# A state-space layer and two feed-forward layers: y of one pair of chunks joined with the next pair's C·B and states, 25 weight shifts on ScalarE, and a new order

## The chip, the cores and the metric

The kernel runs on one core of one Trainium2 chip. The metric is device microseconds of one execution, without a profile, as the median of repeated runs. A second source is one profiled execution, whose hardware trace gives all the rows shown here.

## What is computed

Four sequences of 768 tokens go through a chunked state-space layer (8 heads of 32, state size 16), and its output of 3072 tokens x 256 goes through two feed-forward layers. The first is `elu(x @ w_in) @ w_out` with 2048 inner columns. The second has 1024 inner columns: `(x @ w1) * (x @ w2)`, then `@ w3 @ w_out`. The part that matters here, cut from the reference:

```python
L = exp(cum[..., :, None] - cum[..., None, :]) * causal
M = einsum('bhin,bhjn->bhij', C, B) * L
y = einsum('bhij,bhjd->bhid', M, x)
y += einsum('bhin,bhnd->bhid', C, state) * exp(cum)[..., None]
state = decay_full * state + sum_j(B x decay_from_j)
```

The weights of the feed-forward layers come as 64-bit floats.

## The kernel before

**Chunks and pairs.** The tokens are worked through in 24 chunks of 128 rows, two halves of 64 in each. Four chunks make one tile of 512 tokens. The chunks go in pairs. For each pair but the first two there are two phases of small f32 products on TensorE. `unit_u` (L658) makes C·B of both chunks (`cb_products`, L511, matmuls on L521) and the new parts of the states (`u_products`, L548, L556). `unit_y` (L670) calls `y_products` (L582): M times x (L590, the inner part), then C times state (L598, the state part). The array is divided for them: 32x64 cells for C·B, 64x32 for u and the inner part, 32x32 for the state part. The first four chunks have their own `first_cb`, `first_u` and `first_y`.

**What follows a phase.** After C·B, VectorE multiplies by the decay (`decayed`, L528) and makes the states (`states`, L565). After y, ScalarE (first two tiles) or VectorE copies the result as a rounded high part xTh (`made_x`, L685), and VectorE takes the low part xTl (`take_lo`, L162). Every large product is three matmuls (`mm3`, L382 to L384), low times high, high times low, high times high.

**Rooms in PSUM.** `banks` (L171) gives double banks out of three. A `unit_u` takes two rooms, a `unit_y` two others, and each unit of `x @ w_in` (`unit_a`, L706) one. A room comes free when its last reader is done. The stage of the second layer's `x @ w1` and `x @ w2`, made as sums of products of blocks (`by_product`, L852), has six single banks of its own; there VectorE multiplies two results (`gate_1`, L902, into room_l) and frees a bank for the next product.

**Weights.** A `Piece` (L192) loads 512 KB as pairs of 32-bit words, and makes an f32 of each pair. `shifted` (L209) takes the low word down by 29 bits on VectorE (L210), `scaled` (L213) works on the high word on ScalarE (L214), `joined` (L222) puts them together on VectorE (L224), `his` and `los` make the high and low parts (L236 on ScalarE, L162). There are 44 pieces. The sixteen of w_in and w_out come first, in an order written into `PIECES` (L55), through eight rooms that they take in turn. DMAs of all loads are issued on SP's queue, in program order.

**The order.** `ORDER` (L37) is a string of 1670 letters, written by hand or by a search. Each letter runs the next waiting step of one kind (L1040), and `in_order` (L646) keeps what it issues in that order on every engine. So the order of letters is the order of each engine's queue. The letter v is `half_a` (L701): the first 256 of 512 columns of a unit of `x @ w_in`, kept in `early_h` so that `unit_a` makes the rest alone. The test there is `early = t == 0 and n < len(early_h)`.

Of the kernel before, what the change touches and what calls it, by code (L numbers as in the profile page):

```python
# [37 lines left out]
094AAlU7AlC5Al5UCJCD566l8jCNk5K8JkHND6IjDQjND6KkHNkKQzzYNYzIvzjYNYjkaKjk!HaKXjkxIkNjKarkKMjsHMxKbIrNKxsXrLaHkBjLN8j8vsxX  # L38
BHKuWkPIrbDHMKjkIMKbWINsRXaWHLCNjLBbxCDrCttBjNsCakhVkiyxIrKbXkzsWzMHYYuhKNIaHiXIDbxDNrttjsyVaKzXzkHYYhNVaIxijMrkKbMsHxPL
raINhLjsaxijNhRbxXrLCCiaMSBSBrsBCbshxirLahKBiaxksHrIkbjsxCNKrKuHksbhItDVahtDjijykxirbMKHsMzbzhYPiNYuhKbXHtDtDjkyLaBzIzYY  # L40
INiaxKrXLHbHIsxNkhIRa1jBrMiaCxNCsrKwXxshkNribfsjCXjKHuFhMIatjDHNLIakxCDSiSr1bKxtLNrwsjskykfHFKhIaMzzHKjINibBkMBxYKYbhNri
PsuhbXjDtiXwtkDLykfhFRaHXHIziBNbxIYjLrwzBsNYKukHMfIbjFDMKtHNaDILXCkwxBLCNhtrKajsfjKhiaxiHrkIbFKHxINsrbhskyhSwPjzzYYMKiaH
XSIijMfBakxCFNHCrIaXxsrRwxsrsbfjKkFLahBiuLxbrtBDCHDItbshiKyhHbzXIzYi1CuhYMaDDXttwixMrLBafNLsbBxCFrCkNjsyhazijYkbKxzKr3Y%
&su&h=bitbhtD&D=y=S&Saz=YNziaxYrsaNh3xibxkrrbsshiahjijKbxkK%&ra&s^=hb=&ix&=ar=Nsax1rh3aNxirksb3jxKs@jakK%&=a@#&h3rib&s@&
=x=b=h#Nri^ahs^xia@N#rk#jxsbrKsaSkjSKh%b@i&=xb^h&@=#ahi&ribx#s3r1xsb&=h3^@iar=hbix/srsbh/i|ch_bmi/|#b_/G|e]_gncS[Em({|G}
)]_e>gn<c[*Em(.{G})],<e.>En,g.{*c[,(m)S}*g.1>e.,*G[<3nc,.d*](,mE.}G.{d.,<e],)ng>E,.c{[*dm,(G*.}d.<e]*,d$.d,$),ng>.d+*.(,
[dc,$E}.d@{em,<@d#nG#d*3]g@+)[#^(>E}*c@{e.<dn^dm+d@#G.,)]#*g$>E@(.#^[c{3.d}*m),.e.,G<ng>](,@^E[}c,dm,e.#g.,Gd,*]d{E+n*).
<d.{d[*,(>d)+*c}d+m<e.,2gn>3G[+(]c.}dm,E.3,d.,G.,d,*g{e<dn*)+.(]+2*d.}E.>[d{.c,<2em,).Gn*>g],d.,d.,c[E,md,*({G}*.d<]).e*
>$d,.g*n,c[d.+($,2dm,E.}G.,d]{e$,<)@+gn#d[*(>@E}.*c{e<dn#d.,^)m+d@.g#^@G>.d,@*d+@d#](^.,E[c{*dm}).#G<.>e@#dng]#c[,Em,({G
}g],).,e,*En>d[d+*.d{c<*dm,).+(.*G>.g}.d],<[e+En+2c.,dm{(d}d,G,e]<)$,g.+*dn>2[d,c*.+(.d}*.d,2mE,G*.e{d,n<).,d.>g](,[c,E}  # L50
m*d{e*dnG.)],(.>*d$}E.<g.,d.{[c,<$d+me$,2).g,d+[d>nG.d.d.+c],(mE}d,e{G,nd+]),g<(>.d$[d.Ed{}),<d>,d..,d,dd+++++
# [44 lines left out]
def kernel(  # L96
# [485 lines left out]
    def y_products(*chunks):  # L582
        for k, both in chunks:
            c = ck[k]
            for g in range(2):
                for s in range(SUB):
                    rows = slice(R * s, R * s + R)
                    for q in range(4):
                        h = 2 * q + g
                        T.matmul(both[32 * q:32 * q + 32, s, g], c["x"][rows, D * h:D * h + D], c["L"][rows, h],  # L590
                                 start=g == 0, stop=(k, s) not in state, skip_group_check=True)
        for g in range(2):
            for s in range(SUB):
                for k, both in chunks:
                    for q in range(4) if (k, s) in state else ():
                        at = turned(k, q)
                        rows = slice(32 * at, 32 * at + 32)
                        T.matmul(both[32 * q:32 * q + 32, s, g], state[k, s][rows, D * g:D * g + D], ck[k]["cd"][rows, s, g],  # L598
                                 start=False, stop=True, skip_group_check=True)
# [43 lines left out]

    ends = {}
# [68 lines left out]
    def elu(t, n, h):  # L713
# [9 lines left out]
        if not plain:  # L723
# [4 lines left out]
            yield "i"  # L728
            take_lo(V, lo, e, hi)
# [379 lines left out]
```

## Time and profile before

| | us |
|---|---|
| Median of three runs (526.65 to 526.8) | 526.7 |
| The profiled execution | 524.71 |
| Its span, first to last instruction | 523.0 |
| TensorE (PE) busy | 508.8 |
| VectorE (DVE) busy | 428.8 |
| ScalarE (ACT) busy | 323.6 |
| GpSimd (POOL) busy | 204.4 |

A span is the time from the first to the last instruction of the core. Busy is the union of an engine's instructions, and matmuls overlap, so the starts of matmuls say more of TensorE's pace than their lengths. A wait is put down to the instruction that ended it.

### The profile page before, as it was taken

Reading aid. Unit: us, or ns where it says so; the run is one execution under the profiler, and the core shown is the slowest. Engines: PE = TensorE matmul, PEld = TensorE weight load, DVE = VectorE, ACT = ScalarE, POOL = GpSimd, SP = SyncE. Lnnn points to the kernel's source line nnn. Section 1 sums busy time; section 2 is a strip of 40 time slices with the busy share of each in tenths; the row PEclk is TensorE's granted clock in tenths of the full one; section 3 lists DMA queues with packets and bytes.
Section 4 is the critical chain, followed back from the end, with each engine's and each line's share of the span. In section 5 each row is a group of like instructions: output and inputs, shape, how many; then the busy total and the mean of one; then the engine's idle time right before and its main releaser. Section 6 shows DMA issues by size and latency. Waiting matters only on the chain.

```text
span 523.0 us, 10654 instructions
## 1 busy us (share of the span) xinstructions
PE 508.8 (97%) x4330; PEld 411.2 (79%) x4330; DVE 428.8 (82%) x589; ACT 323.6 (62%) x482; POOL 204.4 (39%) x184
## 2 busy tenths in 40 slices
PE   5799999999999999999999999999989999999996
PEld 3675788778888888878788888888777888888885
DVE  6888989879897996867766797869999989988845
ACT  2585587655754385535476787747766577765650
POOL 3223004205430544122203333967477465755401
PEclk9999999999999999999999999999999999999999
DMA  8993473147555635053202321001000110001002
GB/s 297 348 277 132 134 207 126 41 143 235 170 158 150 222 108 174 1 160 104 69 35 77 106 80 47 35 0 61 0 22 21 61 41 20 1 20 41 21 1 80
DMA packets 28177, 52.66 MB, mean 101 GB/s; under 512 B 2304, under 2 KB 10880, under 8 KB 28128
## 3 DMA queue, kind: packets, MB, share of 16 engines
q1 hardware_dynamic: 27984, 51.85, 30.4%
q8 instruction: 34, 0.56, 0.4%
q14 instruction: 15, 0.12, 0.1%
q10 hardware_dynamic: 144, 0.13, 0.1%
HBM read 45.58 MB, written 6.39 MB: 99 GB/s over the span
## 4 chain that ended last, share of the span: by engine, by line
PE 91%; DVE 6%; issue 1%; DMA 0%; ACT 0%; DVEq 0%
PE acc L382 9%; PE acc L384 9%; PE h L382 9%; PE acc L383 9%; PE h L383 9%; PE h L384 9%; PE p L382 4%; PE p L384 3%; PE p L383 3%; PE acc L745 3%; PE p_d L382 2%; PE p_d L384 2%; PE p_d L383 2%; PE p_E L382 2%; PE p_E L383 2%; PE p_E L384 2%
## 5 line engine op out<-in xcount | busy, mean ns | idle before, releaser
L715 ACT ACTIVATE e<-h 128x1024 f32<-128x1024 f32 x48 | 49.2, 1025 | 58.0 <-PE h L384 55.5
L382 PE MATMUL h<-xTh,w_in 128*128 128x512 f32 (+1 forms) x200 | 80.0, 400 | 0.8 <-ACT xTh L685 0.8
L383 PE MATMUL h<-xTl,w_in 128*128 128x512 f32 (+1 forms) x200 | 77.7, 389 | 0.0
L384 PE MATMUL h<-xTh,w_in 128*128 128x512 f32 (+1 forms) x200 | 77.5, 388 | 0.0
L162 DVE TENSOR_TENSOR g<-e,g 128x1024 fp32r<-128x1024 f32 x44 | 60.1, 1370 | 15.5 <-ACT g L727 15.4
L382 PE MATMUL acc<-g,w_out 128*128 128x512 f32 x176 | 69.6, 396 | 0.0
L722 DVE SCALAR_TENSOR_TENSOR e<-e,h 128x1024 f32<-128x1024 f32 x44 | 53.3, 1214 | 19.7 <-ACT e L717 19.6
L384 PE MATMUL acc<-g,w_out 128*128 128x512 f32 x176 | 68.6, 390 | 0.0
L383 PE MATMUL acc<-g,w_out 128*128 128x512 f32 x176 | 68.5, 389 | 0.0
L727 ACT CAST g<-e 128x1024 fp32r<-128x1024 f32 x44 | 46.2, 1049 | 30.0 <-PE acc L384 26.5
L717 ACT ACTIVATE e<-e 128x1024 f32<-128x1024 f32 x48 | 50.7, 1059 | 0.8
L382 PEld LDWEIGHTS h<-xTh,w_in 128*128 128x128 f32 x200 | 38.6, 193 | 9.4 <-issue 1.8
L383 PEld LDWEIGHTS h<-xTl,w_in 128*128 128x128 f32 x200 | 38.5, 193 | 7.8 <-issue 0.7
L384 PEld LDWEIGHTS h<-xTh,w_in 128*128 128x128 f32 x200 | 38.6, 193 | 7.6
L162 POOL TENSOR_TENSOR w<-raw_wc,w 128x512 fp32r<-128x512 f32 x16 | 23.9, 1502 | 51.5 <-ACT w L236 48.6
L536 POOL TENSOR_TENSOR xbc<-xbc,pr 128x256 f32<-128x256 f32 (+1 forms) x24 | 22.9, 965 | 50.9 <-DMA L<-a_cut 30.7
L382 PEld LDWEIGHTS acc<-g,w_out 128*128 128x128 f32 x176 | 33.0, 188 | 7.4
L384 PEld LDWEIGHTS acc<-g,w_out 128*128 128x128 f32 x176 | 33.0, 188 | 7.0
L383 PEld LDWEIGHTS acc<-g,w_out 128*128 128x128 f32 x176 | 33.1, 188 | 6.6
L504 POOL TENSOR_TENSOR xbc<-xbc,L 128x128 f32<-128x128 f32 x24 | 15.1, 634 | 58.1 <-DVE L L498 37.7
L899 POOL TENSOR_TENSOR room_l<-room_l,room_o 128x512 f32<-128x512 f32 x12 | 19.8, 1647 | 32.8 <-DVE room_o L896 19.1
L498 DVE TENSOR_TENSOR_SCAN L<-L,eye 128x512 f32<-128x512 f32 x20 | 27.3, 1368 | 2.0 <-DMA L<-a_cut 2.0
(427 smaller groups left out, 1278.2 us busy)
## 6 DMA issues: line engine op xcount, KB each, us to landing
xbc<-in_xc SPq DMA_DIRECT2D x24, 512.0 KB, 6.3
raw_wc<-in_w3t SPq DMA_DIRECT2D x16, 512.0 KB, 4.3
L<-a_cut SPq DMA_DIRECT2D x40, 128.0 KB, 4.8
raw_wi<-in_w_in SPq DMA_DIRECT2D x8, 512.0 KB, 8.6
raw_wo<-in_w_out SPq DMA_DIRECT2D x8, 512.0 KB, 6.4
x_dram<-x SPq DMA_DIRECT2D x6, 512.0 KB, 4.9
room_s<-x_dram SPq DMA_DIRECT2D x12, 256.0 KB, 4.3
out_t<-out SPq DMA_DIRECT2D x11, 256.0 KB, 2.0
```

The costliest lines, as they stand in the source:

```text
L162: eng.tensor_tensor(out=lo, in0=raw, in1=hi.bitcast(F32), op=ALU.subtract)
L382: T.matmul(out, wlo, xhi, start=first, stop=False, **kw)
L383: T.matmul(out, whi, xlo, start=False, stop=False, **kw)
L384: T.matmul(out, whi, xhi, start=False, stop=last, **kw)
L498: V.tensor_tensor_scan(out=flat, data0=wide, data1=eye.rearrange("p h s -> p (h s)"), initial=0.0, op0=ALU.mult, op1=ALU.add)
L536: G.tensor_tensor(out=c["cd"][:, n:], in0=c["cd"][:, n:], in1=c["pr"].rearrange("p s (o i) -> p s o i", o=1)[:, n:].to_broadcast([P, SUB - ...
L715: A.activation(e, h, AF.Exp)
L717: A.activation(e, e, AF.Relu, scale=-1.0, bias=1.0)
L722: V.scalar_tensor_tensor(out=gt[t, n] if plain else e, in0=e, scalar=-1.0, in1=h, op0=ALU.mult, op1=ALU.max)
L727: A.copy(hi, e)
L745: T.matmul(acc, word_of(n)[:, j, es], g[:, j], start=m == 0, stop=False)
L899: GATE[m % 2].tensor_tensor(out=s["two"], in0=s["two"], in1=s["u2"], op=ALU.mult)
```

## The change

The y of a pair now takes the whole room that the next pair's C·B and states would have had, and where `JOINED` has a 1 (six of ten pairs of chunks), `unit_u` writes into that same room, and the new `ORDER` has it follow `unit_y` at once. `y_products` makes the state part first, chunk by chunk, and the inner part after it. `unit_u` makes u first and C·B after it. 25 of 44 pieces have their low word shifted by ScalarE. The pieces of w_in and w_out come in another order, and the string `ORDER` is new (the same letters, the same number of each). `POOL_LO` is all zeros and `SCALAR_Z` keeps the old value, so these two change nothing.

```diff
+JOINED = "0100111101"
+SCALAR_Z = 2
+SCALAR_LOW = "11101000001101011001111011011010111100101010"
-PIECES = [(("w_in", "w_out")[k == "o"], "iioiooiiiiooiooo"[:n].count(k)) for n, k in enumerate("iioiooiiiiooiooo")] + [("wo2", m) for m in range(4)] + [("w3", m) for m in range(16)] + [
+PIECES = [(("w_in", "w_out")[k == "o"], "iiioioioiooioioo"[:n].count(k)) for n, k in enumerate("iiioioioiooioioo")] + [("wo2", m) for m in range(4)] + [("w3", m) for m in range(16)] + [
...
         def shifted(self):
-            V.tensor_scalar(self.low, self.low, 29, None, op0=ALU.logical_shift_right)
+            if self.scalar_low:
+                A.activation(self.low, self.low, AF.Copy, scale=15 / 16 * 2.0 ** -29 * (1 - 2.0 ** -8))
+            else:
+                V.tensor_scalar(self.low, self.low, 29, None, op0=ALU.logical_shift_right)
             self.one_of_two()
...
     def y_products(*chunks):
         for k, both in chunks:
+            for g in range(2):
+                for s in range(SUB):
+                    for q in range(4) if (k, s) in state else ():
+                        at = turned(k, q)
+                        rows = slice(32 * at, 32 * at + 32)
+                        T.matmul(both[32 * q:32 * q + 32, s, g], state[k, s][rows, D * g:D * g + D], ck[k]["cd"][rows, s, g],
+                                 start=g == 0, stop=False, skip_group_check=True)
+        for k, both in chunks:
             c = ck[k]
             for g in range(2):
                 for s in range(SUB):
...
-        for g in range(2):
-            for s in range(SUB):
-                for k, both in chunks:
-                    for q in range(4) if (k, s) in state else ():
...
     def unit_u(k):
...
-        rooms = {j: parts_of(banks(f"s{j}")) for j in two}
-        cb_products(*((j, rooms[j][0]) for j in two))
+        rooms = {j: parts_of(joined[j] if JOINED[(k - CPT) // 2] == "1" else banks(f"s{j}")) for j in two}
         for j in two:
             u_products(j, rooms[j][1])
+        cb_products(*((j, rooms[j][0]) for j in two))
...
     def unit_y(k):
-        two = [(j, by_head(banks(f"y{j}")[:, :, :2 * R])) for j in (k, k + 1)]
+        joined.update({j + 2: banks(f"y{j}") for j in (k, k + 1)})
+        two = [(j, parts_of(joined[j + 2])[2]) for j in (k, k + 1)]
...
-094AAlU7AlC5Al5UCJCD566l8jCNk5K8JkHND6IjDQjND6KkHNkKQzzYNYzIvzjYNYjkaKjk!HaKXjkxIkNjKarkKMjsHMxKbIrNKxsXrLaHkBjLN8j8vsxX
+094AAlA75AlUl5UCJCl566kD5jN8DJjCDQ686KNk8jDCkK!NHkKjIHKNQzzYHYNIzvzYkYNjIajkKvMxKkjakPHKrIaNkxsMrLbjMsxjKNrLajXkHsMKjbIH
```

Three places of the order show what the prediction speaks of. The first is on TensorE, the y of chunks 10 and 11 in the kernel before (y10 and y11 are rooms, st states, L the decays):

```order
L590 MATMUL y10_1434<-L10_988,xbc10_940 32x64 x16
L590 MATMUL y11_1435<-L11_1079,xbc11_1059 32x64 x16
L598 MATMUL y10_1434<-xbc10_940,st6_850 32x64 x4
L598 MATMUL y11_1435<-xbc11_1059,st7_853 32x64 x4
L598 MATMUL y10_1434<-xbc10_940,st10_1424 32x64 x4
L598 MATMUL y11_1435<-xbc11_1059,st11_1428 32x64 x4
L598 MATMUL y10_1434<-xbc10_940,st6_850 32x64 x4
L598 MATMUL y11_1435<-xbc11_1059,st7_853 32x64 x4
L598 MATMUL y10_1434<-xbc10_940,st10_1424 32x64 x4
L598 MATMUL y11_1435<-xbc11_1059,st11_1428 32x64 x4
```

The same y with the change, and what stands right behind it:

```order
L597 MATMUL y10_1440<-xbc10_1014,st6_799 32x64 x4
L597 MATMUL y10_1440<-xbc10_1014,st10_1408 32x64 x4
L597 MATMUL y10_1440<-xbc10_1014,st6_799 32x64 x4
L597 MATMUL y10_1440<-xbc10_1014,st10_1408 32x64 x4
L597 MATMUL y11_1441<-xbc11_1033,st7_828 32x64 x4
L597 MATMUL y11_1441<-xbc11_1033,st11_1415 32x64 x4
L597 MATMUL y11_1441<-xbc11_1033,st7_828 32x64 x4
L597 MATMUL y11_1441<-xbc11_1033,st11_1415 32x64 x4
L606 MATMUL y10_1440<-L10_1007,xbc10_1014 32x64 x16
L606 MATMUL y11_1441<-L11_1054,xbc11_1033 32x64 x16
L564 MATMUL y10_1440<-xbc12_1268 32x64 x8
L564 MATMUL y11_1441<-xbc13_1313 32x64 x8
```

The state part now stands ahead of the inner part, and all of chunk 10 ahead of all of chunk 11, where the two took turns by four. The u and C·B of chunks 12 and 13 follow at once, into the rooms y10 and y11; before, some hundred rows lay between.

The second is on TensorE after the unit of `x @ w_in` number 3 of the first tile, before the change (w_in1 is the weight piece of unit 1):

```order
L382 MATMUL h0_3_490<-xTh0_364,w_in3_81 128x512
L383 MATMUL h0_3_490<-xTl0_365,w_in3_81 128x512
L384 MATMUL h0_3_490<-xTh0_364,w_in3_81 128x512
L382 MATMUL h0_1_517<-xTh0_364,w_in1_79 128x256
L383 MATMUL h0_1_517<-xTl0_365,w_in1_79 128x256
L384 MATMUL h0_1_517<-xTh0_364,w_in1_79 128x256
L382 MATMUL h0_1_517<-xTh0_364,w_in1_79 128x256
L383 MATMUL h0_1_517<-xTl0_365,w_in1_79 128x256
```

And with the change, after unit 0 of the first tile:

```order
L390 MATMUL h0_0_381<-xTh0_370,w_in0_78 128x256
L391 MATMUL h0_0_381<-xTl0_371,w_in0_78 128x256
L392 MATMUL h0_0_381<-xTh0_370,w_in0_78 128x256
L390 MATMUL h0_1_417<-xTh0_370,w_in1_79 128x256
L391 MATMUL h0_1_417<-xTl0_371,w_in1_79 128x256
L392 MATMUL h0_1_417<-xTh0_370,w_in1_79 128x256
L390 MATMUL h0_1_417<-xTh0_370,w_in1_79 128x256
L391 MATMUL h0_1_417<-xTl0_371,w_in1_79 128x256
```

Twelve matmuls of 256 columns for unit 1, which stood behind unit 3, are now the first half of unit 1; the second half follows them, also as twelve of 256 columns, and the twelve of 512 columns are gone. Before, unit 1 had been made whole, its early half came later, and no instruction read it.

The third is on ScalarE's queue at the start, before the change, from the copies of the first states (st0) to the last part of x of the first pair:

```order
L572 COPY st0_209<-f2_138 128x128
L572 COPY st1_211<-f2_138 128x128
L214 ACTIVATE raw_wi0_121<-raw_wi0_121 128x512
L236 CAST w_in0_78<-raw_wi0_121 128x512
L572 COPY st2_248<-acc_f_96 128x128
L214 ACTIVATE raw_wi1_123<-raw_wi1_123 128x512
L214 ACTIVATE raw_wo0_125<-raw_wo0_125 128x512
L572 COPY st3_305<-acc_f_96 128x128
L236 CAST w_in1_79<-raw_wi1_123 128x512
L685 CAST xTh0_364<-f2_138 128x2x2x64
L685 CAST xTh0_364<-acc_f_96 128x2x2x64
```

And with the change, from behind the copies of st0 and st1:

```order
L216 ACTIVATE raw_wi0_121<-raw_wi0_121 128x512
L222 ACTIVATE raw_wi0_121<-raw_wi0_121 128x512
L222 ACTIVATE raw_wi1_123<-raw_wi1_123 128x512
L580 COPY st2_289<-acc_f_96 128x128
L580 COPY st3_294<-acc_f_96 128x128
L216 ACTIVATE raw_wi1_123<-raw_wi1_123 128x512
L222 ACTIVATE raw_wi2_125<-raw_wi2_125 128x512
L216 ACTIVATE raw_wi2_125<-raw_wi2_125 128x512
L244 CAST w_in0_78<-raw_wi0_121 128x512
L222 ACTIVATE raw_wo0_216<-raw_wo0_216 128x512
L244 CAST w_in1_79<-raw_wi1_123 128x512
L695 CAST xTh0_370<-f2_138 128x2x2x64
```

Three shifts (L216) stand there that were VectorE's, and the scaling of w_in2 comes ahead of the first copies of x, as that of w_out0 already did. The last row is the first of the same two copies of x; the second follows it.

## Rows read from the trace of the kernel before

**Rows 1.** The page: busy time, share and instructions of each engine

```profile
PE 508.8 (97%) x4330; PEld 411.2 (79%) x4330; DVE 428.8 (82%) x589; ACT 323.6 (62%) x482; POOL 204.4 (39%) x184
```

**Rows 2.** Waits of PE over the run: total us, times, longest us

```profile
PE f L487 <- ACT a_hl L426: 4.4, 1, 4.4
...
PE p L382 <- DVE room_l L902: 1.8, 2, 1.4
```

**Rows 3.** Windows of 20 us: length, PE, PEld, DVE, ACT, POOL busy, clock, DMA

```profile
20.00:40.00 20.00, 19.29 (x141) 15.47 (x144) 16.73 (x27) 15.88 (x25) 3.38 (x6) 1.00 0.94 288
...
360.00:380.00 20.00, 19.55 (x85) 15.42 (x84) 19.97 (x25) 14.24 (x27) 10.54 (x7) 1.00 0.04 12
380.00:400.00 20.00, 18.61 (x81) 14.72 (x80) 19.37 (x23) 13.07 (x25) 14.22 (x10) 1.00 0.09 28
```

**Rows 4.** PE timeline, first big products: start, length, instruction

```profile
20.71 0.55 PE L382 MATMUL h<-xTh,w_in 128*128 128x256 f32 x1 [0.83 <-ACT xTh L685]
...
25.36 0.33 PE L384 MATMUL h<-xTh,w_in 128*128 128x256 f32 x1
...
25.88 0.40 PE L382 MATMUL h<-xTh,w_in 128*128 128x512 f32 x1
...
37.53 0.28 PE L382 MATMUL h<-xTh,w_in 128*128 128x256 f32 x1
...
39.05 0.80 PE L521 MATMUL s<-xbc 32*64 32x128 f32 x32
```

**Rows 5.** PE timeline, a C·B and u phase, then a y phase

```profile
60.38 0.39 PE L384 MATMUL acc<-g,w_out 128*128 128x512 f32 x1
60.70 0.69 PE L521 MATMUL s<-xbc 32*64 32x128 f32 x32
61.32 0.45 PE L556 MATMUL s<-xbc 64*32 64x64 f32 x32
61.70 0.50 PE L382 MATMUL h<-xTh,w_in 128*128 128x512 f32 x1
62.04 0.40 PE L383 MATMUL h<-xTl,w_in 128*128 128x512 f32 x1
62.27 0.40 PE L384 MATMUL h<-xTh,w_in 128*128 128x512 f32 x1
...
67.39 0.86 PE L590 MATMUL y<-L,xbc 64*32 64x64 f32 x64
68.18 0.85 PE L598 MATMUL y<-xbc,st 32*32 32x64 f32 x64
68.96 0.50 PE L382 MATMUL h<-xTh,w_in 128*128 128x512 f32 x1
```

**Rows 6.** PE timeline near the start, and line 598: durations min/median/max

```profile
19.20 0.33 PE L598 MATMUL f<-xbc,st 32*32 32x64 f32 x4
19.23 0.33 PE L598 MATMUL acc_f<-xbc,st 32*32 32x64 f32 x4
19.31 0.33 PE L598 MATMUL f<-xbc,st 32*32 32x64 f32 x4
...
L598 PE MATMUL y<-xbc,st x640: 211/214/239, 56.9 to 257.9; 32*32 32x64 f32 x160
```

**Rows 7.** ScalarE timeline at the start

```profile
12.13 0.43 ACT L572 COPY st<-f 128x128 f32<-128x128 f32 x2 [7.81 <-PE f L556]
...
15.44 0.71 ACT L214 ACTIVATE raw_wi<-raw_wi 128x512 f32<-128x512 f32 x1
16.01 0.70 ACT L214 ACTIVATE raw_wo<-raw_wo 128x512 f32<-128x512 f32 x1
...
20.19 0.38 ACT L685 CAST xTh<-acc_f 128x256 fp32r<-128x256 f32 x1
```

**Rows 8.** Tile raw_wi: durations min/median/max of its two first operations

```profile
L214 ACT ACTIVATE raw_wi<-raw_wi x8: 657/679/709, 12.5 to 43.7; 128x512 f32<-128x512 f32 x8
L210 DVE TENSOR_SCALAR raw_wi<-raw_wi x8: 404/421/612, 13.3 to 53.4; 128x512 uint32<-128x512 uint32 x8
```

More of the change, by code (lines that the diff above doesn't have):

```diff
@@ L42 @@
[L42 to L51, printed above, removed]
+094AAlA75AlUl5UCJCl566kD5jN8DJjCDQ686KNk8jDCkK!NHkKjIHKNQzzYHYNIzvzYkYNjIajkKvMxKkjakPHKrIaNkxsMrLbjMsxjKNrLajXkHsMKjbIH
@@ new lines @@
+KNkBIxLXraLkNKjsaxXKHRrXbxIHCNsrCWIBW8sujCWNaDBhtBDCtkyKkjixuMKbztHNkrIDHXYjIbzthMskYjXaDhKiPLyxNLrBbzsBzHYYjNuIiaMRXbxV
+DrXtWsakMhDtNhKaVjixrVaiHxIsNbxkLrrsBaChsCSiSyjKxVbPrzzHKMYIHsbhXkLNaihBIjYMiCbxXLrBNCsuhLbiRbhkikkaKtHDjItjbDxBKNrKyHK1
+HsIuXzkIYazHDNjItYDaxMthkjNwixKrMrsbXfKHshINajikHFLIaxKNrLwxsjkNrKbkHshIHajINhKBSiCwkSCfjCFiNafxFKHrIbHsBxCyIhkurMbjsMzY
+XDatDNkiwLxhtKbNzHYriIPfajFBXjKhLNkbsiBRyhxuzCrKbjskzaiDYtbxKYrDhaHijItsbxNrhsMwki1bXHHIhXIfajFKSNCSiCaxMrkNaxKsrhwxiLbH
+sBrLfbhFBsIHjikyIhKCuPzYwDMtzYMibfHDXjtkFyKHazMLXYBRbxMrLCXaIzYsBILahxirwxsrhbsNfFiuhaDjNiD1btxkKtjkrasKax%&&hbrBi&=xbs=
@@ new lines @@
+h=Lra&S=sNaxiSrXahsxNirbBksCjCxykCjKrKuhs%bDzDaihYzt3bxYt&r=yi3&&shb&==iah=zNYibxzYajNrks3bxKrkh3sajhKi%&ax=&@irb^#&xs3r
+b1==&h=sNa@SiS1#bx^rN^@sahhika#xi^jjKa@kxK#%rb@sr&s&ah=xirb#@@#&s3b&h==x=ia3^h#ribx/srsbh/i|ch_bmi/|_b/G|e]_gnc[Em({|G})
+]_e>En<g.{*cS,([m)}.G><Se,]1g.d*n,E3[({*.c})m,*e.>G.,gnd.,[c<](,*mE}.G{g.,<)],eE>n*d{.c[,*(.d}.dm,*e.<gn,).,G$>d$](*+.d}
+[d,E$c.{d@,<dm,@)@G#*e>]3#E.*d.,nd+g*{c[d,.^d.+)m#(^@>d.}g@,c@[e#mG<d#*]gn#E[^(3.{G})],<e@>d$,3cn#Em,(.G{d}]),.e*,dn>g*(
++[d<.*c.+Em}d.{*g,e<G,n)]+d.^>(2.E+[c.}d,md.,G{g,e,)n,*d]<d>E*.+c.{2d[*,dm).+(*.>d.2}g.,3<d[+e,dnG2,c],(m,E.}*g{e,d*.d<.
+),$*dn>d[,$G*.d+](,.E}@c{$em,<.G#.)n,d]>d@,d.#g*@+c[(,m^d}g#*E@+G.{e]^#dnE@*(.{).<d^@}[d>.)<#.cem>*@g,nc[#G,d]#(.,dmE}g,
@@ L197, in __init__ @@
             self.lo, self.word, self.parts, self.half = G, None, None, 0
+            self.scalar_low = False
         def load(self):
@@ L590, in y_products @@
                         T.matmul(both[32 * q:32 * q + 32, s, g], c["x"][rows, D * h:D * h + D], c["L"][rows, h],
-                                 start=g == 0, stop=(k, s) not in state, skip_group_check=True)
-        for g in range(2):
-            for s in range(SUB):
-                for k, both in chunks:
-                    for q in range(4) if (k, s) in state else ():
[L596 to L599, printed above, removed]
+                                 start=g == 0 and (k, s) not in state, stop=True, skip_group_check=True)
     def x_room(k):
@@ L642, in first_y @@
             later("X", at_load, CPT + k)
+    joined = {}
     ends = {}
@@ L670, in unit_y @@
     def unit_y(k):
-        two = [(j, by_head(banks(f"y{j}")[:, :, :2 * R])) for j in (k, k + 1)]
+        joined.update({j + 2: banks(f"y{j}") for j in (k, k + 1)})
+        two = [(j, parts_of(joined[j + 2])[2]) for j in (k, k + 1)]
         y_products(*two)
         for j, both in two:
-            later("z", made_x, j, both, A if j < 2 * CPT else V)
+            later("z", made_x, j, both, A if j < SCALAR_Z * CPT else V)
         if k % CPT == 0 and k // CPT + 1 < NTILE:
@@ L727, in elu @@
             A.copy(hi, e)
-            yield "i"
-            take_lo(V, lo, e, hi)
+            pool = POOL_LO[t * NA + n] == "1"
+            yield "T" if pool else "i"
+            take_lo(G if pool else V, lo, e, hi)
     def split_word(n):
@@ L1010 @@
         p.lo = V if 0 < n < VECTOR_LO else G
+        p.scalar_low = SCALAR_LOW[n] == "1"
     for k in range(CPT):
```

6 lines of the change are left out of this document (3 added, 3 removed).

## The prediction

> **What bounds the kernel now.** The page's busy times come first: TensorE is busy 508.8 of 523.0 us, and no other engine over 82% [rows 1]. Then TensorE's waits: the longest are 4.4 us before its first matmul and 1.8 us, in two pieces, for VectorE's L902 [rows 2]. Those two lie between 360 and 400 us, where TensorE is busy 19.55 and 18.61 of 20 us, so that 1.84 us are lost, with VectorE busy 19.97 and 19.37 [rows 3]. The reader is to see that TensorE sets the time almost everywhere: what counts is how much it has to do, how well matmuls follow each other, and when the first large product can start. Lengths hide the second of these, since matmuls overlap, so the timeline is read by starts. Large ones of 512 columns start 0.23 us apart (62.04 to 62.27) [rows 5]. At the start, those of 256 columns take (25.36 - 20.71) / 21 = 0.22 us each, then (25.88 - 25.36) / 4 = 0.13, so TensorE goes at half its pace until 25.4 us, that is at 1.2 GHz and then at 2.4, though the granted clock reads 1.00 in that window [rows 3, 4].
>
> All sums are made against the profiled execution, 524.71 us. The three runs have a median of 526.7, 2.0 us more; I carry the same difference over to them.
>
> **Part 1: the early half of unit 1.** Between 37.53 and 39.05 stand twelve matmuls of 256 columns whose result no one reads [rows 4]. Less the entry into the next phase (0.09, Part 2) they cost 1.52 - 0.09 = 1.43 us. With the change they are used. The price is that unit 1 is now 24 of 256 columns in place of 12 of 512: 24 x 0.12 - 12 x 0.23 = 0.1 us. Sum **-1.3 us**. TensorE has no wait in that stretch that could take it back, other than what Part 4 counts.
>
> **Part 2: six joins.** A phase of small products costs something to enter and to leave. From the last large matmul to the first of C·B are 0.32 us in place of 0.23 (60.38 to 60.70): 0.09. The first large one after a phase takes 0.34 until the next one starts (61.70 to 62.04), 0.11 too much [rows 5]. And before it the array runs empty: the last matmul of L598 starts about 68.18 + 0.85 - 0.21 = 68.82, with 0.21 as the length of one [rows 6], and the next large one at 68.96, 0.14 later, where small ones start 0.02 apart or closer (64 in 0.64 us) [rows 5]. A join saves one exit and one entry, 0.09 + 0.11 + 0.12 = 0.32. From the inner part to u the cells keep their 64x32 shape, so no new gap arises there. Six joins: **-1.9 us**. Below: -1.2, if only the two neighbours of large matmuls are saved; above: -2.0. That u now goes ahead of C·B changes which shape comes last, not how many changes there are; I put nothing, within 0.1 us of each of ten phases either way, since both orders have one entry, one change and one exit.
>
> **Part 3: the state part, one chunk at a time.** This speaks against the change. Near the start, four matmuls of the first chunk (f) start at 19.20, four of the second (acc_f) at 19.23, and the next four of the first at 19.31 [rows 6]. So a cell of the array takes a new pass of 64 columns only 0.11 us after the one before, at half pace, thus 0.055 at full; and the second chunk, whose four cells are others, fits into the same time. A chunk's state part has 16 instructions on four cells, two records each (64 records for two chunks) [rows 5]: eight passes per cell, the last starting 7 x 0.055 = 0.39 after the first, 0.41 with the four side by side. Two chunks by turns needed 0.64 us from first to last start (68.18 to 68.82). One after the other they need 2 x 0.41 = 0.83, if matmuls keep their order. That is 0.19 for each of ten phases: **+1.9 us**. Below 0, if the second chunk overtakes; above +2.4, if each chunk keeps the whole 0.44 of its eight passes. I take the rows' own pace.
>
> Matmuls that keep their order are what the Trainium skill states (TensorE: Matmul & The Clock Gate, Part 3, The mechanism: strict first in, first out in start and end). TensorEngine Tiling (Array Packing), Key Properties, says that different tiles load weights and multiply in parallel; by that alone this term would be 0 and the time 522.0. No row here has a long run on one chunk's four cells, so the trace doesn't decide between them.
>
> **Part 4: the start.** The first large product waits for ScalarE's copy of x, which ends at 20.19 + 0.38 = 20.57 and lets it start at 20.71 [rows 4, 7]. ScalarE's queue up to there is now longer, but it is held up less: it had waited again and again for VectorE, which made shift, joining and scans by turns. From 12.13, where the copies of the first states start, the new queue has the two copies (0.33), nine instructions on pieces (six are shifts and scalings of w_in0 to w_in2, one scales w_out0, two are roundings), two more state copies (0.33), and the two copies of x (0.65). At 0.57 from start to start (15.44 to 16.01) [rows 7] that is 12.13 + 0.33 + 9 x 0.57 + 0.33 + 0.65 = 18.57, 2.0 us sooner. A shift on ScalarE is priced like the scaling of the same size, 0.68 us, since no row shows it [rows 8]. y must be there by then: all C·B stands ahead now, and VectorE makes its four scans and the four decays with one joining between them, so that y of the first pair is due before 17 us. Against it: the copies of states 2 and 3 wait on TensorE with the shift of w_in1 queued behind, and GpSimd makes the last of its products for C ahead of the low part of w_in0. I take **-1.5 us**, between 0 and -2.0. The half pace should last as long as before, and moves along.
>
> **Part 5: what I put at nothing.** The 25 shifts take 25 x 0.42 = 10.5 us off VectorE and put 25 x 0.68 = 17 us on ScalarE [rows 8]. Neither is waited for between 21 and 360 us by more than the 0.83 us at its start [rows 4], and ScalarE has 4.1 us idle even in the full window from 20 to 40 [rows 3]; GpSimd's subtractions for the weights follow ScalarE as before. If that cover were gone, a late rounding would cost about one instruction, 0.66, at the unit that needs it. On SP's queue w_in2 and w_in3 go ahead of w_out pieces, which helps the start; the rows of decays and the next chunks' loads come later, but their first use, the phase of chunks 4 and 5, moves back behind two more units of `x @ w_in`. The joined rooms wait for VectorE's C·B work in place of a fresh pair; see the last rival. In the stage from 360 us the order is new and VectorE as full: I leave its 1.84 us, between 0 and twice that and more.
>
> **Sum.** -1.3 - 1.9 + 1.9 - 1.5 = -2.8: 521.9 for the profiled execution, **523.9** for the median.
>
> **The rivals.**
> A: the second chunk overtakes in the state part. Then Part 3 is 0 and the time 526.7 - 4.7 = 522.0. For it: cells that start 0.03 us apart do work at once [rows 6]. Against it: the matmuls seen there already stood in that order.
> B: the product stage loses more. From 360 to 400 us VectorE has 0.66 of 40 us to spare [rows 3], and its instructions there take 0.7 us or more, so each that is placed one too early before L902 is a wait of that size. With four such, 2.8 us, the gain is gone: 526.7, within 0.2%, about what a measurement can tell from no change.
> C: joined rooms, on the slow side. Of three rooms a joined phase holds two until VectorE has made the low parts, the decays and the states of both chunks, some 3.5 to 4 us by its eight to ten instructions of 0.3 to 0.7. Cover is the rest of the phase, 1.0 us (60.70 to 61.70) [rows 5], and one unit in the third room, 12 x 0.23 = 2.7. The sum is even, so it decides whether one longer VectorE instruction of a unit stands ahead: then TensorE waits about 1 us. For it: six joins in a stretch where VectorE is 80% busy. Against it: after four of the joins a unit on the accumulators stands first, which needs no room. At all six, 6 x 0.9 = 5.4: 526.7 - 2.8 + 5.4 = 529.3.
>
> **How the numbers follow.** The forecast has 0.42, with a range of its own from 522.8 to 525.4; A has 0.25, B 0.18, C 0.15. The forecast and A are faster by over 0.2% (1.05 us, so below 525.65): 0.67. B is the same, 0.18; C slower, 0.15. The range reaches from 521.0 (A with the full gain at the start and half the waits of the product stage gone) to 527.2, which leaves out most of C.
>
> **What would show it.** Right: the first product of `x @ w_in` starts near 19.2 us; no twelve lone matmuls after unit 3; from y to u no large gap, and 14 phases in place of 20; L597's 64 records take about 0.83 us from first to last start in place of 0.64; a shift on ScalarE takes 0.6 to 0.7 us; TensorE waits for L913 (the old L902) about 2 us. Wrong: L597 still in 0.64 (then A); waits of `x @ w_in` for VectorE's L536 or L573 behind joined phases (C); waits from 340 us on above 4 us (B); a first product that starts at 20.7 or later.

## The result and the profile after

Against the kernel before on the same chip the changed kernel took 534.13 us in the median of five runs (531.18 to 534.55), the kernel before 526.65: a ratio of 1.0141, with a 95% interval from 1.012 to 1.0163. It is 7.5 us slower. The forecast was 523.9, with a range up to 527.2. The profiled execution took 531.18 us, its span is 529.5.

The page of the changed kernel: busy times, and the DMA queue that, as worked out below, carries TensorE's instructions. A queue's row has packets, MB and share.

```profile
PE 508.9 (96%) x4330; PEld 412.5 (78%) x4330; DVE 411.7 (78%) x564; ACT 336.1 (63%) x507; POOL 200.8 (38%) x184
...
q8 instruction: 34, 0.56, 0.5%
```

VectorE has lost 17 us and ScalarE gained 13 [rows 1 for before]. The shifts make the 13 and 10 of the 17: in the last experiment, which puts all of them back on VectorE, ScalarE has 12.7 less and VectorE 10.0 more than with them on ScalarE (323.3 and 423.6 against 336.0 and 413.6). TensorE has the same busy time in a span that is 6.5 us longer. So it waits, and the waits of PE say where (us in total, times, longest):

```profile
PE y L529 <- issue: 3.9, 3, 1.4
PE acc_f L606 <- issue: 2.2, 1, 2.2
PE y L564 <- issue: 1.8, 1, 1.8
PE acc_f L597 <- POOL xbc L544: 1.0, 1, 1.0
...
PE p L390 <- DVE room_l L904: 0.5, 1, 0.5
```

The wait of the product stage, which [rows 2] had at 1.8, is down to 0.5. New are waits inside joined phases (L529, L564: lines of C·B and u that write into y) and at the start (L606), and their releaser is "issue": the engine waited for nothing that the profile shows. Two joined phases on PE's timeline, the one near 56 us without such a wait and the one near 118 with it:

```profile
56.18 0.99 PE L597 MATMUL y<-xbc,st 32*32 32x64 f32 x64
...
57.76 0.53 PE L564 MATMUL y<-xbc 64*32 64x64 f32 x32
58.22 0.69 PE L529 MATMUL y<-xbc 32*64 32x128 f32 x32
...
118.45 0.99 PE L597 MATMUL y<-xbc,st 32*32 32x64 f32 x64
119.37 0.81 PE L606 MATMUL y<-L,xbc 64*32 64x64 f32 x61
...
120.02 0.54 PE L564 MATMUL y<-xbc 64*32 64x64 f32 x31
120.49 0.43 PE L529 MATMUL y<-xbc 32*64 32x128 f32 x5
122.14 0.68 PE L529 MATMUL y<-xbc 32*64 32x128 f32 x27 [1.22 <-issue]
122.75 0.50 PE L390 MATMUL h<-xTh,w_in 128*128 128x512 f32 x1
```

TensorE stops after the fifth of 32 like records, in the middle of a loop, where nothing new is read or written. That speaks against data. What such a place can lack is its own instructions. Counted in the trace in program order, each TensorE instruction has a number (weight loads, matmuls and the few semaphore instructions, from 0). The stops stand at 448 (start), 3008, 3777, 4289 and 5056, and a small one of 0.39 us near 69 us at 1728. Each is 192 or 193 above a multiple of 256. And TensorE's 2 x 4330 + 68 = 8728 instructions over the 34 packets above, of 16384 bytes each, are 256.7 a packet. So TensorE's program seems to arrive in blocks of 256, that is 128 matmuls with their loads, and TensorE to stop at the end of a block; the experiments test it. The packets' own times, for the four long stops (us):

| phase | block begins | packet for the next one | its end reached | goes on |
|---|---|---|---|---|
| 118.45 | 118.87 | 119.85 to 120.73 | 120.65 | 122.14 |
| 156.16 | 156.64 | 157.42 to 158.43 | 158.40 | 159.88 |
| 177.18 | 177.51 | 178.20 to 179.61 | 179.05 | 181.03 |
| 217.84 | 218.20 | 219.02 to 220.00 | 219.74 | 221.38 |

The packet starts 0.7 to 1.0 after its block begins, takes 0.9 to 1.4, and TensorE goes on 1.4 after its end: 3.2 to 3.5 in all. In these phases 128 small matmuls are run in 1.5 to 1.8. The difference is the stop. The phase at 56.18 has its boundary at matmul 77 of 192, so the block that begins there is not used up inside the phase.

At the start the same thing (a stop of 2.19 in the profile's count, 2.5 from start to start) meets a chain:

```profile
14.97 0.67 PE L606 MATMUL acc_f<-L,xbc 64*32 64x64 f32 x22
17.84 0.45 PE L606 MATMUL acc_f<-L,xbc 64*32 64x64 f32 x10 [2.19 <-issue]
18.76 0.65 PE L597 MATMUL f<-xbc,st 32*32 32x64 f32 x16 [0.48 <-ACT st L580]
20.44 0.65 PE L597 MATMUL acc_f<-xbc,st 32*32 32x64 f32 x16 [1.03 <-POOL xbc L544]
...
22.84 0.55 PE L390 MATMUL h<-xTh,w_in 128*128 128x256 f32 x1 [0.64 <-ACT xTh L695]
```

The first large product starts at 22.84 in place of 20.71 [rows 4]. The two rows in the middle wait for copies of states (L580) and for a product of GpSimd that needs them.

Of the 6.5 us in span, 2.1 lie ahead of the first large product. From there to the end it is 529.5 - 22.84 = 506.6 against 523.0 - 20.71 = 502.3, 4.4 more. From start to start the four stops are 1.49 + 1.49 + 1.98 + 1.65 = 6.6; without them and the 0.39 the rest would be 2.6 shorter than before.

### The profile page after: what moved, and what is told of

It reads as the page before. It is cut to its first block, busy times and chain, and to the rows that moved or that the text cites. A ratio compares the mean times of both kernels' runs of the same rounds, so it can differ in the third digit from the quotient of the medians.

```text
span 529.5 us, 10635 instructions
## 1 busy us (share of the span) xinstructions
PE 508.9 (96%) x4330; PEld 412.5 (78%) x4330; DVE 411.7 (78%) x564; ACT 336.1 (63%) x507; POOL 200.8 (38%) x184
## 4 chain that ended last, share of the span: by engine, by line
PE 93%; DVE 3%; issue 2%; DMA 1%; ACT 1%; SPq 0%; DVEq 0%
PE acc L390 9%; PE acc L391 9%; PE acc L392 9%; PE h L390 8%; PE h L391 8%; PE h L392 8%; PE p L390 4%; PE p L391 4%; PE p L392 4%; PE acc L756 3%; PE p_E L391 2%; PE p_E L390 2%; PE p_E L392 2%; PE p_d L390 2%; PE p_d L391 2%; PE p_d L392 2%
## 5 line engine op out<-in xcount | busy, mean ns | idle before, releaser
L390 PE MATMUL h<-xTh,w_in 128*128 128x512 f32 (+1 forms) x200 | 78.4, 392 | 0.6 <-ACT xTh L695 0.6
L392 PE MATMUL h<-xTh,w_in 128*128 128x512 f32 (+1 forms) x200 | 76.8, 384 | 0.0
L166 DVE TENSOR_TENSOR g<-e,g 128x1024 fp32r<-128x1024 f32 x44 | 58.5, 1329 | 12.3 <-ACT g L737 12.3
L512 POOL TENSOR_TENSOR xbc<-xbc,L 128x128 f32<-128x128 f32 x24 | 12.3, 514 | 100.4 <-DVE L L506 69.6
L544 POOL TENSOR_TENSOR xbc<-xbc,pr 128x256 f32<-128x256 f32 (+1 forms) x24 | 22.1, 935 | 13.3 <-DVE pr L472 12.9
L895 ACT COPY room_o<-p 128x512 f32<-128x512 f32 x24 | 14.1, 588 | 19.0 <-PE p L392 18.7
```

What stands on the lines that cost most here:

```text
L166: eng.tensor_tensor(out=lo, in0=raw, in1=hi.bitcast(F32), op=ALU.subtract)
L390: T.matmul(out, wlo, xhi, start=first, stop=False, **kw)
L392: T.matmul(out, whi, xhi, start=False, stop=last, **kw)
L544: G.tensor_tensor(out=c["cd"][:, n:], in0=c["cd"][:, n:], in1=c["pr"].rearrange("p s (o i) -> p s o i", o=1)[:, n:].to_broadcast([P, SUB - ...
L895: A.copy(s["u2"], rooms[m % 2])
```

## The experiments

Theory S: the supply of instructions stops TensorE, by where block boundaries fall. Rival D: the joined phases wait for data, a room or another engine's result that the profile doesn't name.

### Boundaries moved by added work

```diff
+PAD = {10: 38}
...
+        for i in range(PAD.get(k, 0)):
+            j, p, s = two[i // 8 % 2], i // 2 % 4, i % 2
+            c, rows, to = ck[j], slice(R * s, R * s + R), turned(j, p)
+            T.matmul(rooms[j][1][32 * to:32 * to + 32, s], c["bd"][rows, 2 * p:2 * p + 2].rearrange("p h n -> p (h n)"),
+                     c["x"][rows, 64 * p:64 * p + 64], start=True, stop=True, skip_group_check=True)
         cb_products(*((j, rooms[j][0]) for j in two))
```

> The changed kernel, with 38 small products of u (76 records of TensorE, 152 instructions with their weight loads) made once more in the phase of chunks 10 and 11 near 106 us; they write the same values again. Theory S (supply of instructions): TensorE's instructions come in blocks of 256, and a block is there some 3.3 us after the one two before it was left; the four stops of 1.5 to 2.0 us in joined phases stand where a block ends that was run through in 1.6 us. The 76 records move every later block boundary 76 matmuls ahead: in the phases that start near 118, 156, 177 and 218 us the first boundary in the phase then stands at about matmul 86, 95, 77 and 82 in place of 38, 46, 24 and 34, and the block before it holds large matmuls. So all four stops go, none of over 0.5 us comes up later: about 6.6 less and 0.6 for the added work, 528.1 in place of 534.1. Rival D (data: the u and C B of a joined phase wait for a room or for what VectorE or GpSimd make): the stops stay at the same products, and the time is 534.7.

Measured: 526.66 us, ratio to the kernel before 1.0011 (0.9993 to 1.0028): 7.5 less than the changed kernel, with more work. Theory S had 6.0 less. That is what the profiled executions show (531.18 and 525.17); the medians give 1.5 more, which the theory does not explain. The same phase, now near 119 us:

```profile
118.61 0.39 PE L393 MATMUL acc<-g,w_out 128*128 128x512 f32 x1
...
120.50 0.54 PE L565 MATMUL y<-xbc 64*32 64x64 f32 x31
120.97 0.69 PE L530 MATMUL y<-xbc 32*64 32x128 f32 x32
121.59 0.50 PE L391 MATMUL h<-xTh,w_in 128*128 128x512 f32 x1
121.93 0.39 PE L392 MATMUL h<-xTl,w_in 128*128 128x512 f32 x1
```

All four stops are gone, and no wait for "issue" is left but the one at the start. No instruction of those phases was touched: rival D falls.

The same with `PAD = {4: 24}`:

> The changed kernel, with 24 small products of u (48 records) made once more in the phase of chunks 4 and 5 near 52 us. Theory S: boundaries move 48 matmuls ahead from there on. The joined phase at 56 us, which has no stop, gets one of about 1.5 us near its matmul 157; those near 118, 177 and 218 lose theirs (boundary 10 to 24 large matmuls ahead of the phase); the one near 156 keeps one, near matmul 126 in place of 174; the one near 275, which has none, gets one near matmul 139. Three stops in place of four, in other places: about 1 us less time than the changed kernel. Rival D: stops stay where they are, 0.4 us more time.

Measured, in the profiled execution alone: 529.73. The phase without a stop has one:

```profile
59.13 0.86 PE L607 MATMUL y<-L,xbc 64*32 64x64 f32 x64
59.79 0.52 PE L565 MATMUL y<-xbc 64*32 64x64 f32 x28
62.05 0.30 PE L565 MATMUL y<-xbc 64*32 64x64 f32 x4 [1.75 <-issue]
```

64 + 64 + 28 = 156 matmuls into the phase, where 157 was expected. The stops near 118, 177 and 218 went, as expected. Those expected near 156 and 275 did not come: there the boundary lies 1.5 matmuls ahead of the phase, or 11 into it, and the packets began at 156.79 and 271.03, 3.1 and 2.2 before the phases (159.88 and 273.27). That is 2.8 and 2.4 before TensorE reached the boundary (159.56 and 273.43): in these two stretches of large matmuls the next block came early, and my rule had not allowed for that. The time is 1.45 below the changed kernel's profile, where one stop in place of five, less the added work, would give some 4.6. The first large product came 1.0 later (23.86), and part of the rest is the clock (next experiment).

### The same in the kernel before

```diff
+        for i in range(64 if k in (10, 14) else 0):
...
```

(the loop of the experiments above, behind `u_products`)

> The kernel before, where no phase is joined, with 64 small products of u (128 records) made once more in two of its phases of C B and u: those of chunks 10 and 11 (near 113 us) and of chunks 14 and 15 (near 162 us). Both phases then have 192 records, and 128 records are one block of 256 instructions, so the later boundaries keep their places. Theory S: the phase near 113 has a boundary 14 large matmuls ahead of it and gets no stop; in the phase near 162 a block of 128 records that begins at matmul 32 is run through in about 1.2 us, so TensorE stops near matmul 160 for 1.5 to 2.0 us. Rival D: the same added work costs the same at both places, about 1.0 us each, since there is no joined room to wait for.

Measured, in the profiled execution alone: 533.1. The two padded phases (L669 is the added line):

```profile
115.16 1.56 PE L669 MATMUL s<-xbc 64*32 64x64 f32 x128
116.66 0.50 PE L382 MATMUL acc<-g,w_out 128*128 128x512 f32 x1
...
162.91 0.69 PE L521 MATMUL s<-xbc 32*64 32x128 f32 x32
...
163.81 1.28 PE L669 MATMUL s<-xbc 64*32 64x64 f32 x97
167.89 0.46 PE L669 MATMUL s<-xbc 64*32 64x64 f32 x31 [2.80 <-issue]
168.28 0.50 PE L382 MATMUL acc<-g,w_out 128*128 128x512 f32 x1
```

32 + 32 + 97 = 161, where 160 was expected. The same products cost 1.5 us at one place and 4.5 at the other, with no joined room in the kernel. The stop is longer than expected (3.0 from start to start): its packet began 2.05 after the boundary, not 0.7 to 1.0. Theory S is shown: a stop came where the count of instructions puts it, and went where the count moved it away. What the theory lacked is when the next block is asked for, hence the two misses of the run before.

A stop can cost more than its own length. From 169.4 us on, 1.5 after TensorE went on, the granted clock is at the lower of its two levels (1.2 GHz) for 3.4 us, and large products start 0.43 apart in place of 0.23. A window with its PE clock (the 0.51), and two starts:

```profile
169.40:172.90 3.50, 3.50 (x11) 2.71 (x10) 3.46 (x7) 0.00 (x0) 0.00 (x0) 0.51 0.00 0
171.32 0.63 PE L382 MATMUL acc<-g,w_out 128*128 128x512 f32 x1
171.74 0.63 PE L383 MATMUL acc<-g,w_out 128*128 128x512 f32 x1
```

Half of 3.4, or 1.7 us, is lost on top. Such a stretch stands also behind the stop of the run with 24 repeated products (63.2 to 66.6) and in two runs below. Not every stop has one behind it: the changed kernel's profile has four long stops and no such stretch.

### Joined phases taken apart

In the order, the letter u of each joined pair is put behind the next letter a or b, a unit of large matmuls (`uMKb` becomes `MKbu`, and the like, six times; a D and a t go with it once).

> The changed kernel with u and C B of each joined pair one unit of large matmuls later (12 of 512 columns, 2.7 us); rooms stay joined. Theory S: the unit between gives the supply its time, no stop of over 0.5 us is left in these phases (6.9 less), and six more entries and exits of a phase cost about 0.3 each: 534.1 - 6.9 + 1.8 = 529.0. If the stops came from TensorE being held in a joined phase by its rooms, they would move to the u phase: 534.1 or more.

Measured: 534.28 (ratio 1.0154, 1.0118 to 1.019), no gain. The stops in the joined phases are gone, but other waits took their place. Near 228 us the work that now stands between y and u had been all the work between that u and the next y, which needs its states:

```profile
227.96 0.69 PE L529 MATMUL y<-xbc 32*64 32x128 f32 x32
230.11 0.65 PE L597 MATMUL y<-xbc,st 32*32 32x64 f32 x32 [1.45 <-DVE st L573]
231.46 1.00 PE L597 MATMUL y<-xbc,st 32*32 32x64 f32 x29 [0.70 <-DVE st L573]
```

A unit of `x @ w_in` waited 1.8 for the same states, and the start's stop was 3.9 in this profile. The clock was at its lower level twice for 3.4 us, from 129.1 and from 231.5, behind these waits: 3.4 us lost. The run doesn't say what six joins are worth; the phases' lengths do (below).

### The start

The first 48 letters of the order:

```diff
-094AAlA75AlUl5UCJCl566kD5jN8DJjCDQ686KNk8jDCkK!N
+094AAlA75AlUl5UCJCl566kD5jN8DJjCD66Q8KNk8jDCkK!N
```

> The changed kernel with ScalarE's copies of the states 2 and 3 ahead of the first y in the order of the start, in place of behind it. Theory: at the start a stop of 2.5 us (15.3 to 17.8) holds the first y, the copies wait for the end of that y since they stand behind it and read the same bank, and GpSimd's products for the second y wait for the copies. Then the copies come near 15 us, the stop itself stays, and the first product of x @ w_in starts near 20.7 in place of 22.84: 2.1 less, 532.0. Rival: what follows the stop on TensorE or ScalarE's queue (the shifts and scalings of weights ahead of the copies of x) decides alone: the first product stays near 22.8 and the time at 534.1.

Measured: 533.08 (ratio 1.0112, 1.0069 to 1.0154); the profiled execution took 529.44. In its profile:

```profile
15.64 0.67 PE L606 MATMUL acc_f<-L,xbc 64*32 64x64 f32 x22
17.49 0.44 PE L606 MATMUL acc_f<-L,xbc 64*32 64x64 f32 x10 [1.18 <-issue]
17.86 0.33 PE L597 MATMUL f<-xbc,st 32*32 32x64 f32 x4
...
20.23 0.55 PE L390 MATMUL h<-xTh,w_in 128*128 128x256 f32 x1 [0.55 <-ACT xTh L695]
```

The waits for L580 and L544 behind the stop are gone (one of 0.42 for L580 now stands ahead of it) and the first product starts at 20.23, where 20.7 was expected; the stop stays, but 1.0 shorter. The median gained 1.05, half of what was expected, and the two intervals overlap. The four stops of the joined phases are still there, and behind the last one the clock is at its lower level from 218.4 to 221.8 us. The stop's length differs from profile to profile of the same opening, so one start says little. Kernels that open like the one before stopped for 0.9, 2.8 and 3.0 us and reached the first product at 20.71, 22.49 and 22.59. Those that open like the changed one stopped 2.5, 2.5, 3.8 and 3.9 and reached it at 22.84, 22.55, 23.86 and 23.84. The profile that the forecast was made from had the shortest stop of all fourteen.

### The early half alone

The kernel before, with the second letter v of its order left out, and so the twelve matmuls that no one reads:

> The kernel before without the second early half, whose result no one reads (the second v of the order, twelve matmuls of 256 columns). Forecast's Part 1: 1.4 less, 525.2 in place of 526.65, ratio 0.9973. Rival: the room that the dead half took came free at once and nothing waited for TensorE there, so VectorE or ScalarE, not TensorE, sets that stretch and no more than 0.3 is saved.

Measured: ratio 0.9957 (0.9941 to 0.9973), 524.36 against 526.27. In the profile the first product comes late (22.49, by the start's stop); from there to the end it is 500.95 in place of 502.26: 1.3 less, though its first 24 products of 256 columns, at the half pace of the start, took 5.50 us in place of 5.17. The medians give 1.9. The forecast's Part 1 holds, if anything on the low side.

### Both mends together, and the state part

The 38 repeated products and the earlier copies:

> The changed kernel with both: the 38 repeated products in the phase of chunks 10 and 11, and the copies of the states 2 and 3 ahead of the first y. Theory: the two do not touch each other, so no stop over 0.5 us after the start, a first product of x @ w_in near 20.3, and 526.66 - 2.0 = 524.7, below the kernel before (526.65). Rival: the earlier start is given back later (product stage or weights), 526.6.

Measured: 523.73, ratio 0.9959 (0.9943 to 0.9975): below both kernels. The theory's 524.7 lies 1.0 above. No stop over 0.5 us is left behind the start, as expected; but the first product starts at 21.64, where 20.3 was expected, since the start's stop was 2.9 here. So the start gave less than the theory had, and the total more; why is open.

Then the state part by turns:

```diff
-        for k, both in chunks:
-            for g in range(2):
-                for s in range(SUB):
+        for g in range(2):
+            for s in range(SUB):
+                for k, both in chunks:
                     for q in range(4) if (k, s) in state else ():
```

> As the run before this one, and the state part takes its two chunks by turns again, as the kernel before had it (now ahead of the inner part). Forecast's Part 3, as the trace of the changed kernel corrects it: the 64 records of a state part go from 0.777 back to about 0.64 us from first to last start, 0.13 for each of ten phases, 1.3 less: 523.4. Rival: the inner part behind it, which runs chunk by chunk, gives it back (its first products then wait for cells), and the phase is as long as before: 524.7.

Measured: 524.11 (0.9948 to 0.9981), no gain. In the profile all ten state parts are at 0.64 us from first to last start in place of 0.78, but two y phases, near 66 and 220 us, stop for 0.6 and 1.5. Three runs were to tell why.

With `PAD = {10: 41}`:

> The run with the state part by turns (524.11), with 41 repeated products in place of 38. In that run's profile the phase near 220 us stops for 1.5 us at its matmul 112: the block that ends there came late, since its transfer began 3.9 us after the boundary before it. Six records more put that boundary six large matmuls, 1.4 us, further ahead of the phase. Theory S: this stop goes and the state part's 1.3 shows: 522.8 or less. Rival: the turns give nothing back, 523.7 to 524.1 as the two runs before.

With one load of that kernel later on SP's queue:

> The run with 41 repeated products and the state part by turns (524.2), with one 512 KB load of a chunk (issued at 215.5 us, just ahead of the y phase that stops for 1.4 us near 219) put behind the next rows of the decays on SP's queue, so that it is issued near 221 us, after that phase. Theory: the block of instructions that this phase needs is asked for near 214 and its transfer begins only at 219.5, when the load's share of the DMA engines (0.7 to 1.1 from 216 to 219) is through; without the load the transfer begins before 217, the stop goes, and the time is 1.2 less, 523.0. Rival: transfers of instructions don't wait for loads; the transfer still begins 4 us late and the stop stays, 524.2.

With states of that kernel earlier on VectorE:

> The run with 41 repeated products and the state part by turns (524.2), with VectorE's two instructions for the states of chunk 19 moved ahead of the rounding, the two low parts and the decay product that stood before them (near 215 us). In three profiles with the turns the transfer of the block that the y phase of chunks 18 and 19 needs began 1.07 to 1.09 us after these states were done, and the phase's fifth record waits for them. Theory W (the next block is asked for by TensorE's sequencer when it passes a certain place some 25 to 48 matmuls behind a boundary, so a wait that stands ahead of that place holds the request too): the states are done about 2 us sooner, the transfer begins 1.5 us sooner or more in respect to the phase, and the stop of 1.4 us near 219 goes or falls below 0.4: 1.2 less, 523.0. Rival: the request comes from the boundary or from the transfers' own queue; the transfer still begins some 4.4 us behind the boundary and the stop stays, 524.2.

Measured: 524.2, 525.67 and 525.31 us, the ratios 0.9977 (0.9958 to 0.9996), 0.9989 (0.9966 to 1.0012) and 0.9989 (0.9968 to 1.0009). All three missed: the stop stayed at 1.40, 1.54 and 1.42. In the second the DMA engines were at a share of 0.01 and 0.00 from 218 to 220 us, and the packet still began at 220.92: loads didn't hold it. In the third the states were done early and the decay product last:

```profile
216.28 1.09 DVE L574 SCALAR_TENSOR_TENSOR st<-st,pr,y 128x64 f32<-128x64 f32 x4
...
219.21 0.68 DVE L537 TENSOR_TENSOR L<-y,L 128x512 f32<-128x512 f32 x1
```

```profile
220.69 0.85 PE L598 MATMUL y<-xbc,st 32*32 32x64 f32 x64
221.47 0.68 PE L607 MATMUL y<-L,xbc 64*32 64x64 f32 x42
223.35 0.42 PE L607 MATMUL y<-L,xbc 64*32 64x64 f32 x22 [1.20 <-issue]
```

The packet began at 221.02, 1.13 after the end of that L537 (219.89). In the three other profiles with turns it began 1.10 to 1.13 after the end of the last of chunk 19's VectorE instructions, there the states (219.05 and 220.18; 218.40 and 219.52; 219.82 and 220.92). In the program the first record of the second chunk carries one wait for all of VectorE's work on that chunk, states and decay product. So my edit had moved the wrong instruction, and in four profiles the packet began only once that wait was over. With turns, it stands at the phase's ninth record; chunk by chunk, at its 33rd, and there the packet began at 218.50, 1.3 before the phase (219.84). So the four times point to the wait as what holds the request; a run in which both instructions come early was not made, so it is not shown.

### The shifts

The run with both mends, all 25 shifts back on VectorE (`SCALAR_LOW` all zeros):

> The run with the 38 repeated products and the earlier copies (523.73), with all 25 shifts back on VectorE, in the same places of the order. Forecast's Part 5: covered by TensorE's work on both engines, so no change over 0.5, 523.2 to 524.2. Rival: the shifts take 25 x 0.42 = 10.5 us of VectorE back, in the first 180 us where it is busy 80 to 90%, and TensorE waits for its low parts and decays: 1 to 3 us more.

Measured: 524.73, ratio 0.9978 (0.9963 to 0.9994), against 0.9959 (0.9943 to 0.9975) with the shifts on ScalarE. That is 1.0 more, above the expected range and at the foot of the rival's; but the intervals overlap, and its profile has two stops of 0.4 and 0.6 at block boundaries of the y phases near 67 and 222. So whether the shifts on ScalarE gain anything by themselves stays open.

## Why the prediction was wrong

The parts of the sum that count TensorE's own work held within some 0.6 us each. The sum fell on one thing that no part had: TensorE's program has to arrive, too. The profiled execution took 9.3 more than the 521.9 forecast for it: 7.0 are stops in the phases and 3.6 the start (Part 4), less 1.6 by which the rest came out better (0.5 in Part 3 and 1.3 in the product stage, less 0.2 in Part 2); 0.3 stay unexplained.

- **Part 1**, the early half: -1.3, measured -1.3 in the profile behind the start, -1.9 between the medians.
- **Part 2**, six joins, -1.9, is the step that failed, not in what it counted but in what a join costs. From the matmul ahead of a phase to the second large one after it, less two of 0.227, the boundary experiment's profile gives 121.93 - 118.61 - 0.454 = 2.87 for a joined phase, and for y and u alone the rows below give 95.06 - 92.69 - 0.454 = 1.92 and 74.05 - 72.36 - 0.454 = 1.24. A join saves 0.29, where 0.32 was forecast. But it makes 176 or 192 small matmuls in a row, more than a block, and four of six cost 1.5 to 2.0 in stops.

```profile
72.36 0.39 PE L393 MATMUL acc<-g,w_out 128*128 128x512 f32 x1
...
74.05 0.40 PE L392 MATMUL h<-xTl,w_in 128*128 128x512 f32 x1
...
92.69 0.39 PE L393 MATMUL h<-xTh,w_in 128*128 128x512 f32 x1
...
95.06 0.39 PE L392 MATMUL acc<-g,w_out 128*128 128x512 f32 x1
```

- **Part 3**, the state part: right in kind, +1.9 forecast. From first to last start a state part takes 0.99 - 0.21 = 0.78 in place of 0.64 [rows 5]: 0.14 for each of ten, 1.4. The second chunk does not overtake, so rival A falls; for the order of matmuls the trace agrees with the page of the Trainium skill that the forecast named for it, with 0.78 where the two chunks side by side had 0.64. The 0.14 bought something that the forecast did not see: the first chunk's part does not wait for the second chunk's data, and with turns the next block came too late.
- **Part 4**, the start: -1.5 forecast, +2.1 in the profiles, about +0.9 between the middle starts of three and four profiles (22.49, and 23.34 between the two middle ones). ScalarE's own work is as forecast: from 12.59 to the end of the copies of x at 22.69, less one wait of 3.63, it is 6.5, and the sum had 18.57 - 12.13 = 6.4. The wait is what the sum lacked: the copies of states 2 and 3 had been moved behind the first y, that y stopped for its instructions, and GpSimd and the second y came after. "Against it: the copies of states 2 and 3 wait on TensorE" was in the text, without a price.

```profile
18.35 0.43 ACT L580 COPY st<-acc_f 128x128 f32<-128x128 f32 x2 [3.63 <-PE acc_f L606]
```

- **Part 5** and the product stage: its waits fell from 1.8 to 0.5 (B is wrong, and it is better than the nothing that I put). TensorE is busy throughout in both windows, where [rows 3] had 19.55 and 18.61:

```profile
360.00:380.00 20.00, 20.00 (x90) 16.57 (x89) 17.87 (x24) 15.12 (x29) 13.88 (x9) 1.00 0.12 40
380.00:400.00 20.00, 20.00 (x88) 15.99 (x87) 19.05 (x25) 14.89 (x28) 13.67 (x9) 1.00 0.04 14
```

- **Rival C** had the right place and the wrong cause: no unit waits for VectorE behind a joined phase. That its 529.3 is the nearest to the measured time is chance.

The trace of before held the hint: a stop at instruction 449. The first y at the start stood still for 0.9 us (16.81 to 17.71, in the waits as 0.6 for "issue"):

```profile
17.71 0.31 PE L598 MATMUL f<-xbc,st 32*32 32x64 f32 x1 [0.60 <-issue]
```

Behind the start its phases have at most 128 matmuls, and none of them stopped. Phases of 128 are no sure cover: they did stop in other profiles, for 0.4 us near 69 us in the changed kernel and for up to 1.5 with turns. The Trainium skill (Runtime: NRT & Kernel Launch, Instruction fetch mechanics) says that programs come in 16 KiB blocks of 256 instructions, and calls the cost of a boundary "mostly hidden". The size agrees with the stops' distances here. That the cost is hidden does not hold here where a block was run through in 1.5 to 1.8 us and the next one took 3.2 to 3.5.

Open is why the changed kernel's median lies 3.0 above its profiled execution, and the kernel before's 2.0 above its own: the other executions have no trace. The start's stop, 0.9 to 3.0 and 2.5 to 3.9, can give 1 to 2 of it. For the changed kernel the clock is a likely part: its profiled execution has a mean granted clock of 0.999, the four others 0.995, 0.997, 0.997 and 0.999. In the profiles one stretch of 3.4 us at the lower level goes with a mean of 0.996 or 0.997, and costs 1.7 us. The execution with 0.999 took 534.04 all the same, so this is not the whole. Open, too, is what sets the length of the start's stop: its packet began between 14.98 and 16.96 us in fourteen profiles, while the DMA engines were full (a share of 1.02 to 1.08 from 12 to 18 us in the changed kernel), but no run changed their load there.

## What to carry to other kernels

Count instructions where matmuls are small: a weight load and a matmul each take a place, and 128 pairs in a row that run faster than the next block arrives made TensorE stop at the block's end here, whatever the data did. A wait with "issue" as its releaser in the middle of a loop, at the same remainder of the instruction count each time, is the sign; added matmuls that shift the remainder test it, and can even win. Since any edit ahead of such a run moves its boundaries, keep dense runs well below 128 matmuls (phases of 64 stopped in none of the fourteen profiles, phases of 128 behind the start in six), or compare two versions only after both profiles have been searched for such stops.

## What the runs showed of the hardware

- TensorE's instructions come as packets of 16384 bytes on a DMA queue of their own. Around the stops in joined phases a packet starts 0.6 to 1.2 us after the boundary ahead of it (2.05 in the padded kernel before) and takes 0.9 to 1.4; TensorE goes on 1.2 to 1.6 after its end.
- The packet can start well ahead of the boundary that TensorE is about to reach (by 2.4 us at 273 us in the experiment with 24 repeated products), or 3.8 to 4.4 behind it, in the four runs with turns, where a semaphore wait on TensorE's queue stands shortly after it.
- Work added at one of two like places cost 1.5 us at the one and 4.5 at the other.
- Behind some stops and waits (1.7 to 3.0 us from start to start), and not behind others like them, the granted clock was at its lower level for 3.4 us: in four of fourteen profiles, twice in one of them.
